# Sevenths for the middle tile: x w_in in a fused retention and two-expert kernel

## The chip, the cores and the metric

One core of one Trainium2 chip. The metric is device time in microseconds (us) for one execution. Everything is float32; the matrix products are made of three float32r products each (below).

## What is computed

A retention layer gives 1536 tokens of width 512. Two feed-forward layers follow. The change lies in the second one, in its first product (`x @ w_in`) and what takes that product's result:

```
def _moe_ref(x, w_a, w_b, w_out):      # x 1536x512, w_a, w_b 512x1536, w_out 1536x512
    return (x @ w_a) * (x @ w_b) @ w_out
def _moe2_ref(x, w_in, w_out):         # x 1536x512, w_in 512x2048, w_out 2048x512
    h = x @ w_in
    g = np.maximum(0.01 * h, h)
    return g @ w_out
x = attention(q, k, v); x = _moe_ref(x, ...); return _moe2_ref(x, ...)
```

## The kernel before

**Tiles.** Everything is held transposed: features on the 128 partitions, 512 tokens along the free axis. The tokens form three tiles, t = 0, 1, 2; t = 1 is the middle one. `y[t, kc]` is x of the second layer (four blocks of 128 features), `w_in` comes in 16 blocks of 128 columns ("wi", f), and `g[t, f]` is the result. Each operand of a product is split into a high and a low float32r part, and `mm3` makes three matmuls: high by high, high by low, low by high. Each matmul loads its own 128x128 weights. SBUF tiles of 128x512 come from a pool of 83 (`Slots`).

**Pairs.** From f = 2 on, blocks of `w_in` are taken in seven pairs, one pair in each round q = 1 to 7 (f = 2q, 2q + 1). In `seven_for_eight` the tiles 0 and 2 are the two rows of a 2x2 block product (features in two halves, columns in two blocks), done in Winograd's way with seven block products for eight. Each is six matmuls of 512 columns; they gather in the PSUM banks `top`, `left` and `mid`. Sums of inputs are formed beforehand (`SY` for x, the "twisted" weights for w_in). The middle tile goes the plain way: `middle` makes 12 matmuls of 512 columns for each of the two blocks, in the banks `pa` and `pb`. A pair has 66 matmuls of 512 columns.

**Order.** `seven_for_eight` is a generator in three parts. In round q the program writes out: the first part of pair q (half of `pa`), the third part of pair q - 1, one product of the next stage (`make2`: six matmuls of 512 columns and six of 256, into three banks `blk` that are held until round 7), and the second part of pair q. Between the products it calls `pump`, which takes work from a queue (rounding of weights, splits, sums of weights, operand forms of the next stage) by nominal cost until the stated time is used up. Every engine executes in the order in which the program writes out, so `pump` decides what stands ahead of what on VectorE and ScalarE.

**Who reads PSUM.** ScalarE copies `top` before the next product is added on the same bank (`s1` L1419, `uu` L1442, `u3` L1431), and makes g by a leaky ReLU (`leaky`, lines 1387 and 1389). VectorE adds `left` and `mid` to earlier copies (`total`, L1423); the ReLU of such sums is done later by `summed`. For the middle tile before, `straight` makes g from `pa` and `pb` at once, two ScalarE instructions of 256 columns each.

**Room.** g tiles that would not fit are sent to DRAM by POOL (`Away.send`, L776) and brought back by SP (L790). This holds for t = 2, and for f from 8 on. Rounding a weight block takes three ScalarE instructions (lines 327, 329, 331) and three of VectorE.

Of the kernel before, what the change touches and what calls it, by code (L numbers as in the profile page):

```python
# [20 lines left out]
P = 128  # L21
# [34 lines left out]
FORM2 = ((), (0,), (1,), (2,), (3,), (4,), (5,), (6, 7))  # L56
MAKE2 = ((), (0,), (1,), (2,), (3,), (4,), (5,), (6, 7))
NMADE2 = 8
LEAD1 = 4
PARK = (0, 0, 0, 0, 0, 1, 1, 1, 2, 1, 1, 2)  # L60
WITH = ((), (), (), (0,), (1,), (2,), (3,), (4,), (5,), (6,), (7, 8, 9), (10, 11))
# [169 lines left out]
def retention_moe_kernel(ctx: ExitStack, tc: tile.TileContext, ins, out):  # L231
# [14 lines left out]
    def as32(t):  # L246
        return t.bitcast(F32)
# [144 lines left out]
        queue.extend(items[2:])  # L392

    def enqueue_split(key, keep=False, far=False):
        def high():
            weights[key] = slots.new(F32R, f"{key[0]}{key[1]}h"), slots.new(F32R, f"{key[0]}{key[1]}l")
            (nc.vector.tensor_copy if key[0] == "wi" and key[1] > 1 else nc.scalar.copy)(weights[key][0], rounded[key])

        def low():
            src = rounded.pop(key)  # L400
            if far:
                nc.scalar.mul(weights[key][1], as32(weights[key][0]), -1.0)
                nc.gpsimd.dma_start(weights[key][1], src, accum_op=ALU.add)
            else:
                nc.vector.tensor_sub(weights[key][1], src, as32(weights[key][0]))
            if keep:
                kept[key] = src
            else:
                slots.done(1)

        behind.extend([(0.05, high), (0.05 if far else 0.61, low)])
# [42 lines left out]
    def twisted(key):  # L454
        return ("t" + key[0], key[1])
# [372 lines left out]
    def seven_for_eight(ka, kb, X, S, xf, ends):  # L828
# [58 lines left out]
        slots.done(4)  # L887
        slots.tick()

    def fast(f):  # L890

        mul, add = nc.vector.tensor_mul, nc.vector.tensor_add
        for t in range(NTILE):
            h[t, f] = slots.new(F32, f"h{t}{f}")
        u = []

        def uu(top):
            u.append(slots.new(F32, f"u{f}"))
            nc.scalar.copy(u[0], top)

        def mb(pb):
            mul(h[1, f], h[1, f], pb)
# [12 lines left out]
        return seven_for_eight(("a", f), ("b", f), x, S, xf, (  # L915
            lambda top: nc.scalar.copy(h[0, f], top),
            lambda left: add(h[0, f], h[0, f], left),
            lambda pa: signed(h[1, f], pa, 1),
            uu,
            lambda top: nc.scalar.copy(h[2, f], top),  # L920
            lambda mid: add(h[2, f], h[2, f], mid),
            mb, c21, c12,
        ))

    y = {}

    def once(cache, kind, f):

# [369 lines left out]
    def y_leave(i, o, parts, with_, op, banks):  # L1298
        sums = banks
        if op:  # L1300
            sums = {m: slots.new(F32, f"yc{i}{o}{m}") for m in parts}
            for m in parts:
                op(sums[m], with_[m], banks[m])

        def onto(d, x):
            nc.gpsimd.dma_start(yf[d], yf[x], accum_op=ALU.add)

        def leave_part(m):
            y_split(i, o, m, sums[m])
            while turn:  # L1310
                t, n = turn.pop(0)
                nc.scalar.mul(yf[t, n], yf[t, n], -1.0)
                if n < 2:
                    onto((2, 2 + n), (2, n))
                    onto((2, n), (0, n))
            if m == 2 and o and not i:
                for j in range(2):
                    onto((0, j), (2, 2 + j))
            if m < 2:
                if not op:  # L1320
                    yf[0, m] = slots.new(F32, f"yf{m}")
                    nc.scalar.copy(yf[0, m], sums[m])
                else:
                    yf[2 * i, 2 * o + m] = sums[m]
                    if i:
                        turn.append((2, 2 * o + m))
                    else:
                        onto((0, 2 + m), (0, m))
            elif op:
                slots.done(1)  # L1330

        for m in parts:
            if op and len(parts) == 3:

                queue.append((0.65, lambda m=m: leave_part(m)))
            else:
                leave_part(m)
# [67 lines left out]
        if f == FF2 - 1:  # L1405
            slots.done(2 * KC)

    sums2 = []

    def summed():  # L1410
        while sums2:
            t, f = sums2.pop(0)
            leaky(g[t, f], g[t, f], t)
            gs.send(t, f)

    def fast2(f):

        def s1(top):
            nc.scalar.copy(g_new(0, f), top)  # L1419
            summed()  # L1420
# [12 lines left out]

        def c21(top):
            straight(2, f, top)
            summed()

        return seven_for_eight(("wi", f), ("wi", f + 1), y, SY, yf, (
            s1,
            lambda left: total(0, f, left),  # L1440
            lambda pa: straight(1, f, pa),
            lambda top: nc.scalar.copy(g_new(0, f + 1), top),  # L1442
            u3,
            lambda mid: total(2, f + 1, mid),
            lambda pb: straight(1, f + 1, pb),
            c21,
            lambda mid: total(0, f + 1, mid),
        ))
# [42 lines left out]
            z.soon.clear()  # L1491

    spare.extend(mixed_items(yf, SY, "r", True))
    before = None
    for q in range(HALF):
        f = 2 * q
        for key in (("wi", f + 2), ("wi", f + 3)) if q + 1 < HALF else ():
            if key in dram:
                obtain(key)
            if key not in rounded:  # L1500
                enqueue_round()
            enqueue_split(key, q + 1 in PAIRS)
        forms = list(FORM2[q])
        for n in range(max(NWQ[q], len(forms))):
            if n < NWQ[q]:
                enqueue_round()
            if n < len(forms):
                queue.append((0.0, lambda m=forms[n]: queue.__setitem__(slice(0, 0), z.items(m))))
        queue.extend(behind)
        behind.clear()  # L1510
        if q + 1 in PAIRS:
            queue.extend(sub_items(("wi", f + 2), ("wi", f + 3)))
        if q in PAIRS:
            now = fast2(f)
            next(now)
            if before:
                next(before, None)
            make2(MAKE2[q - 1])
            next(now)
            before = now  # L1520
            if q == HALF - 1:
                for m in range(LEAD):
                    queue.append((0.34, lambda m=m: z.early(m)))
                queue.extend(z.items(NMADE2))
                next(now, None)
                slots.done(16 + 6 * KC)
# [118 lines left out]
```

## Time and profile before

| | us |
|---|---|
| median of 3 runs | 556.27 (555.9 to 557.31) |
| the profiled execution | 555.79 |
| its span on the core | 554.0 |
| TensorE busy in the span | 548.2 (99%) |
| VectorE, ScalarE busy | 460.3 (83%), 385.8 (70%) |

The pairs of the second layer run from 330 to 448 us of the span. The profile's busy TensorE counts from a matmul's start to its modelled end; the distance between starts shows its pace. The chain of work that ended last is TensorE for 93% of the span.

### The profile page before, as it was taken

How to read it: one execution, taken by the hardware profiler on the slowest of the kernel's cores; microseconds unless marked ns; L12 is line 12 of the kernel's file. 1: busy time of each engine (PE TensorE's matmuls, PEld its weight loads, DVE VectorE, ACT ScalarE, POOL GpSimd, SP SyncE). 2: the span in 40 equal slices, each digit the busy share in tenths (PEclk: the TensorE clock that was granted, in tenths of full speed). 3: DMA queues.
4: the chain of work that ended last, by engine and by line, in shares of the span. 5: the costliest groups of instructions: out<-in, count | busy, mean ns of one | idle time of the engine just before them, and what ended most of it. 6: DMA issues, size and time to landing. Idle time of an engine off the chain costs nothing.

```text
span 554.0 us, 10490 instructions
## 1 busy us (share of the span) xinstructions
PE 548.2 (99%) x3742; PEld 462.0 (83%) x3742; DVE 460.3 (83%) x973; ACT 385.8 (70%) x797; POOL 157.3 (28%) x202
## 2 busy tenths in 40 slices
PE   8999999999999999999999999999999999999997
PEld 5878888888888888788888888888888888888886
DVE  4978968888898898898779869896977798999862
ACT  4876477787779888867657557769766886687800
POOL 3435101113232331266620230221433556600000
PEclk9999999999999999999999999999999999999999
DMA  8999834548698987899993362665777799964111
GB/s 308 353 359 239 214 95 133 155 133 213 175 259 236 243 234 237 269 305 236 234 189 96 57 134 76 180 182 164 240 232 228 209 272 241 222 165 119 59 58 57
DMA packets 49765, 108.19 MB, mean 195 GB/s; under 512 B 5936, under 2 KB 13360, under 8 KB 49712
## 3 DMA queue, kind: packets, MB, share of 16 engines
q1 hardware_dynamic: 27504, 66.80, 36.6%
q0 software_dynamic: 22064, 40.64, 34.4%
q8 instruction: 29, 0.48, 0.3%
q14 instruction: 24, 0.20, 0.1%
q10 hardware_dynamic: 144, 0.08, 0.1%
HBM read 73.68 MB, written 18.35 MB: 166 GB/s over the span
## 4 chain that ended last, share of the span: by engine, by line
PE 93%; DMA 4%; ACT 1%; DVE 0%; SPq 0%; issue 0%
PE blk L259 12%; PE blk L258 12%; PE blk L260 12%; PE top L258 6%; PE top L259 6%; PE top L260 5%; PE pa L258 4%; PE pa L260 4%; PE pa L259 4%; PE pb L258 4%; PE pb L260 4%; PE pb L259 4%; PE mid L258 3%; PE mid L260 3%; PE mid L259 3%; DMA n<-in_kn 2%
## 5 line engine op out<-in xcount | busy, mean ns | idle before, releaser
L259 PE MATMUL blk<-form,form 128*128 128x512 f32 (+1 forms) x224 | 75.8, 339 | 0.0
L258 PE MATMUL blk<-form,form 128*128 128x512 f32 (+1 forms) x224 | 75.6, 337 | 0.0
L260 PE MATMUL blk<-form,form 128*128 128x512 f32 (+1 forms) x224 | 75.3, 336 | 0.0
L174 DVE TENSOR_TENSOR form<-g,form 128x512 fp32r<-128x512 f32 x112 | 57.7, 553 | 1.0 <-DMA out<-c 0.2
L259 PE MATMUL blk<-forma,forma 128*128 128x512 f32 (+1 forms) x168 | 56.9, 338 | 0.0
L258 PE MATMUL blk<-forma,forma 128*128 128x512 f32 (+1 forms) x168 | 56.7, 337 | 0.0
L168 ACT CAST form<-g 128x512 fp32r<-128x512 f32 x112 | 52.3, 513 | 6.1 <-DVE form L174 3.8
L260 PE MATMUL blk<-forma,forma 128*128 128x512 f32 (+1 forms) x168 | 56.4, 336 | 0.0
L174 DVE TENSOR_TENSOR forma<-h,forma 128x512 fp32r<-128x512 f32 x84 | 43.1, 553 | 5.7 <-ACT forma L168 4.0
L258 PEld LDWEIGHTS blk<-form,form 128*128 128x128 f32 x224 | 42.5, 190 | 5.3
L259 PEld LDWEIGHTS blk<-form,form 128*128 128x128 f32 x224 | 42.5, 190 | 4.7
L260 PEld LDWEIGHTS blk<-form,form 128*128 128x128 f32 x224 | 42.3, 189 | 4.8
L168 ACT CAST forma<-h 128x512 fp32r<-128x512 f32 x84 | 38.9, 511 | 8.3 <-DMA h<-h 8.3
L776 POOL DMA_DIRECT2D farg<-g x26 | 15.7, 617 | 79.6 <-ACT g L1389 61.7
L147 POOL DMA_DIRECT2D h<-h x33 | 32.8, 1131 | 15.1 <-DVE h L906 4.9
L258 PEld LDWEIGHTS blk<-forma,forma 128*128 128x128 f32 x168 | 31.9, 190 | 4.0
L259 PEld LDWEIGHTS blk<-forma,forma 128*128 128x128 f32 x168 | 31.9, 190 | 3.6
L260 PEld LDWEIGHTS blk<-forma,forma 128*128 128x128 f32 x168 | 31.7, 189 | 3.6
L776 POOL DMA_DIRECT2D farh<-h x19 | 11.0, 578 | 74.9 <-DVE h L906 50.6
L174 DVE TENSOR_TENSOR form<-wq,form 128x256 fp32r<-128x256 f32 x56 | 23.6, 421 | 10.0 <-ACT form L168 9.9
L168 ACT CAST form<-wq 128x256 fp32r<-128x256 f32 x56 | 22.6, 404 | 5.1 <-PE blk L259 2.4
L147 POOL DMA_DIRECT2D g<-farg x22 | 22.1, 1054 | 7.7 <-DVE form L174 5.1
(3061 smaller groups left out, 1679.5 us busy)
## 6 DMA issues: line engine op xcount, KB each, us to landing
raw_wi<-in_w SPq DMA_DIRECT2D x16, 512.0 KB, 4.4
raw_wq<-in_w SPq DMA_DIRECT2D x16, 512.0 KB, 4.8
farg<-g POOLq DMA_DIRECT2D x26, 256.0 KB, 4.4
g<-farg SPq DMA_DIRECT2D x26, 256.0 KB, 6.7
raw_a<-in_wab SPq DMA_DIRECT2D x12, 512.0 KB, 4.1
raw_b<-in_wab SPq DMA_DIRECT2D x12, 512.0 KB, 4.7
raw_wo<-in_wo SPq DMA_DIRECT2D x12, 512.0 KB, 4.7
g<-farg POOLq DMA_DIRECT2D x20, 256.0 KB, 8.7
```

The lines of the kernel that those rows point to most:

```text
L147: queue.append((0.0, lambda piece=piece: self.nc.gpsimd.dma_start(self.A(*d[1:], j)[piece], self.A(*x1[1:], j)[piece], accum_op=ALU.add)))
L168: nc.scalar.copy(h, src)
L174: nc.vector.tensor_sub(*todo.pop(0))
L258: nc.tensor.matmul(ps, w[0], x[0], start=first, stop=False, skip_group_check=more)
L259: nc.tensor.matmul(ps, w[0], x[1], start=False, stop=False, skip_group_check=more)
L260: nc.tensor.matmul(ps, w[1], x[0], start=False, stop=last, skip_group_check=more)
L776: nc.gpsimd.dma_start(self.far[t, f], self.tiles[t, f])
```

## The change

In rounds q = 2 to 7 the middle tile is done in Winograd's way as well, by itself: its 512 tokens are the two rows of the 2x2 product, 256 each. Its seven products are six matmuls of 256 columns each, in banks `intop`, `inleft` and `inmid`; they replace the 24 matmuls of `middle`. The second block of a pair is then used in one half only, so its high and low parts share one tile. The middle tile's fp32 values (`ym`) are kept until sums of them are formed and split (`inner_items`). Its results are now sums, so the ReLU comes late: `in_c21` does it at the end of the pair, for all sums waiting. Six tiles of g (t = 0, 1 and f = 5, 6, 7) go to DRAM and are recalled in rounds 5 (f = 5) and 7 (f = 6, 7).

```
+INNER = 2
+LENT = {5: 5, 6: 7, 7: 7}
     def enqueue_split(key, keep=False, far=False):
+        part = slice(QT, TT) if key[0] == "wi" and key[1] % 2 and key[1] > 2 * INNER else slice(0, TT)
...
+    def inner_items(last):
...
+    def seven_in_all(ka, kb, ends, inner):
...
+        want(*ka)
+        in_top = bank("intop")[:, 0:QT]
+        product(in_top, ka, 0, token(X0, 0), True, False)
+        ms1(in_top)
+        yield
+        top, left = bank("top"), bank("left")
+        product(top, ka, 0, [y[0, 0], y[0, 1]], True, False)
+        s1(top)
+        product(left, ka, 1, [y[0, 2], y[0, 3]], True, False)
+        pump(2.0)
+        c11(left)
+        left = bank("inleft")[:, 0:QT]
+        product(left, ka, 1, token(X1, 0), True, False)
+        mc11(left)
+        pump(0.7)
+        until(lambda: not ym)
...
+        product(in_top, tb, 1, SM[2], False, True)
+        muu(in_top)
+        product(top, tb, 1, [SY[2, 0], SY[2, 1]], False, True)
+        uu(top)
+        mid = bank("mid")
+        product(mid, ta, 0, [SY[1, 0], SY[1, 1]], True, False)
+        m1(mid)
+        in_mid = bank("inmid")[:, 0:QT]
+        product(in_mid, ta, 0, SM[1], True, False)
+        mm1(in_mid)
+        pump(3.3)
+        product(in_top, tb, 0, SM[3], False, True)
+        mc22(in_top)
+        product(top, tb, 0, [SY[3, 0], SY[3, 1]], False, True)
+        pump(0.6)
+        c22(top)
...
+        pump(0.7)
+        yield
+        product(in_mid, kb, 1, SM[4], False, True)
+        pump(0.6)
+        mc12(in_mid)
+        product(mid, kb, 1, [SY[4, 0], SY[4, 1]], False, True)
+        pump(1.3)
+        c12(mid)
+        product(in_top, ta, 1, token(X1, 1), False, True)
+        mc21(in_top)
+        product(top, ta, 1, [y[2, 2], y[2, 3]], False, True)
+        c21(top)
+        pump(1.0)
...
             elif op:
-                slots.done(1)
+                ym[i, o] = sums[m]
+            else:
+                ym[i, o] = slots.new(F32, "ym")
+                nc.scalar.copy(ym[i, o], sums[m])
...
+    def sent(t, f):
+        gs.send(t, f)
+        if t < 2 and f in LENT:
+            lent[t, f] = park.tile([P, TT], F32, tag=f"lent{t}{f}", name=f"lent{t}{f}")
+            nc.gpsimd.dma_start(lent[t, f], g.pop((t, f)))
+            slots.done(1)
+    def recall(f):
+        for t in range(2):
+            nc.sync.dma_start(g_new(t, f), lent.pop((t, f)))
     def summed():
         while sums2:
             t, f = sums2.pop(0)
             leaky(g[t, f], g[t, f], t)
-            gs.send(t, f)
+            sent(t, f)
+        while sums3:
+            f, i = sums3.pop(0)
+            bend(g[1, f][:, i * QT:(i + 1) * QT], g[1, f][:, i * QT:(i + 1) * QT], i)
...
+        def in_c21(ps):
+            bend(part(f, 1), ps, 1)
+            summed()
+            for i in range(2):
+                sent(1, f + i)
...
         if q in PAIRS:
+            for n in LENT:
+                if LENT[n] == q:
+                    recall(n)
+            if q == INNER:
+                while spare:
+                    spare.pop(0)[1]()
+                queue[0:0] = inner_items(True)
             now = fast2(f)
```

## Rows read from the trace of the kernel before

**Rows 1.** The page: busy time by engine, and the clock in 40 slices.

```profile
PE 548.2 (99%) x3742; PEld 462.0 (83%) x3742; DVE 460.3 (83%) x973; ACT 385.8 (70%) x797; POOL 157.3 (28%) x202
...
PEclk9999999999999999999999999999999999999999
```

**Rows 2.** Waits of PE, whole span: us in total, times, longest; the longest.

```profile
PE warm L986 <- PEq L1634: 0.8, 1, 0.8
```

**Rows 3.** Busy time of one round (q = 3), by engine; clock, DMA share, GB/s.

```profile
363.95:381.01 17.06, 17.06 (x81) 14.23 (x79) 14.13 (x30) 11.78 (x24) 3.01 (x5) 1.00 0.52 143
```

**Rows 4.** Timeline of PE: start, duration, instruction; a stretch of 512 columns.

```profile
349.64 0.39 PE L258 MATMUL pa<-y10h,wi4h 128*128 128x512 f32 x1
...
361.88 0.39 PE L258 MATMUL blk<-form,form 128*128 128x512 f32 x1
```

**Rows 5.** Timeline of PE: 18 matmuls of 256 columns, then of 512.

```profile
307.28 0.28 PE L258 MATMUL blk<-forma,forma 128*128 128x256 f32 x1
...
309.43 0.40 PE L258 MATMUL blk<-forma,forma 128*128 128x512 f32 x1
...
310.82 0.39 PE L258 MATMUL blk<-forma,forma 128*128 128x512 f32 x1
```

**Rows 6.** Tile blk: weight loads, ns min/median/max.

```profile
L258 PEld LDWEIGHTS blk<-form,form x224: 187/188/192, 344.6 to 550.3; 128*128 128x128 f32 x112
```

**Rows 7.** Timeline of PE at the turn to the last round (q = 7).

```profile
426.04 0.39 PE L258 MATMUL pa<-y00h,wi14h 128*128 128x512 f32 x1
...
429.89 0.39 PE L260 MATMUL mid<-r41h,wi13l 128*128 128x512 f32 x1
...
436.30 0.39 PE L258 MATMUL top<-r20h,twi15h 128*128 128x512 f32 x1
```

**Rows 8.** Timeline of ACT at the same turn; in brackets idle before and its releaser.

```profile
426.24 0.38 ACT L1387 ACTIVATE g<-pb 128x256 f32<-128x256 f32 x1 [0.24 <-PE pb L260]
426.52 0.38 ACT L1389 ACTIVATE g<-pb 128x256 f32<-128x256 f32 x1
426.78 0.66 ACT L327 ACTIVATE wq<-raw_wq 128x512 f32<-128x512 f32 x1
...
431.53 0.61 ACT L1389 ACTIVATE g<-top 128x512 f32<-128x512 f32 x1
432.02 0.65 ACT L1389 ACTIVATE g<-g 128x512 f32<-128x512 f32 x1
432.54 0.69 ACT L327 ACTIVATE wq<-raw_wq 128x512 f32<-128x512 f32 x1
...
435.47 0.62 ACT L1419 COPY g<-top 128x512 f32<-128x512 f32 x1
```

**Rows 9.** Timeline of ACT at the turn to round 6.

```profile
409.72 0.66 ACT L327 ACTIVATE wi<-raw_wi 128x512 f32<-128x512 f32 x1
...
413.37 0.57 ACT L1389 ACTIVATE g<-top 128x512 f32<-128x512 f32 x1
...
416.72 0.59 ACT L1419 COPY g<-top 128x512 f32<-128x512 f32 x1 [0.38 <-PE top L260]
```

**Rows 10.** VectorE adds out of PSUM, ns min/median/max: 512 columns, 256 columns.

```profile
L1423 DVE TENSOR_TENSOR g<-g,mid x14: 678/682/689, 341.8 to 446.0; 128x512 f32<-128x512 f32 x14
...
L1472 DVE TENSOR_TENSOR c<-up,blk x4: 414/420/422, 517.3 to 551.0; 128x256 f32<-128x256 f32 x4
```

**Rows 11.** Timeline of DVE: the idle stretch of round 1, the sum of the last turn.

```profile
332.65 0.43 DVE L345 TENSOR_SCALAR wq<-wq 128x512 f32<-128x512 f32 x1 [3.08 <-ACT wq L327]
...
433.12 0.68 DVE L1423 TENSOR_TENSOR g<-g,mid 128x512 f32<-128x512 f32 x1
```

**Rows 12.** DMA issues, KB, median us to landing.

```profile
farg<-g POOLq DMA_DIRECT2D x26, 256.0 KB, 4.4
g<-farg SPq DMA_DIRECT2D x26, 256.0 KB, 6.7
```

**Rows 13.** The SP queue's own waits, 300 to 500 us: total, times, longest.

```profile
SPq L464 <- DMA farg<-g: 17.0, 2, 12.9
```

More of the change, by code (lines that the diff above doesn't have):

```diff
@@ L394, in enqueue_split @@
     def enqueue_split(key, keep=False, far=False):
+        part = slice(QT, TT) if key[0] == "wi" and key[1] % 2 and key[1] > 2 * INNER else slice(0, TT)
         def high():
-            weights[key] = slots.new(F32R, f"{key[0]}{key[1]}h"), slots.new(F32R, f"{key[0]}{key[1]}l")
-            (nc.vector.tensor_copy if key[0] == "wi" and key[1] > 1 else nc.scalar.copy)(weights[key][0], rounded[key])
+            if part.start:
+                both = slots.new(F32R, f"{key[0]}{key[1]}")
+                weights[key] = both[:, 0:QT], both[:, QT:]
+            else:
+                weights[key] = slots.new(F32R, f"{key[0]}{key[1]}h"), slots.new(F32R, f"{key[0]}{key[1]}l")
+            (nc.vector.tensor_copy if key[0] == "wi" and key[1] > 1 else nc.scalar.copy)(
+                weights[key][0], rounded[key][:, part]
+            )
         def low():
@@ L404, in low @@
             else:
-                nc.vector.tensor_sub(weights[key][1], src, as32(weights[key][0]))
+                nc.vector.tensor_sub(weights[key][1], src[:, part], as32(weights[key][0]))
             if keep:
@@ L888, in seven_for_eight, with minus_both, high, low @@
         slots.tick()
+    def inner_items(last):
+        sub, add = nc.vector.tensor_sub, nc.vector.tensor_add
+        def minus_both(d, a, b):
+            nc.vector.scalar_tensor_tensor(d, a, -1.0, b, op0=ALU.mult, op1=ALU.subtract)
+        for op, d, a, b in (
+            (minus_both, (1, 1), (1, 0), (1, 1)), (sub, (1, 0), (0, 0), (1, 0)),
+            (add, (0, 0), (0, 0), (1, 1)), (add, (0, 1), (0, 1), (0, 0)),
+        ) if not last else ():
+            yield 0.69, lambda op=op, d=d, a=a, b=b: op(ym[d], ym[a], ym[b])
+        for n, key in ((3, (1, 0)),) if last else ((1, (1, 1)), (2, (0, 0)), (4, (0, 1))):
+            def high(n=n, key=key):
+                if n == 3:
+                    SM[n] = [tuple(part[:, QT:] for part in y[1, j]) for j in range(2)]
+                else:
+                    hi, lo = slots.new(F32R, f"m{n}h"), slots.new(F32R, f"m{n}l")
+                    SM[n] = [(hi[:, c], lo[:, c]) for c in (slice(0, QT), slice(QT, TT))]
+                for j in range(1 + (n == 3)):
+                    c = slice(j * QT, (j + 1) * QT) if n == 3 else slice(0, TT)
+                    nc.scalar.copy(SM[n][j][0] if n == 3 else hi, ym[key][:, c])
+                SM[n, 0] = None if n == 3 else (hi, lo)
+            def low(n=n, key=key):
+                whole = SM.pop((n, 0))
+                src = ym.pop(key)
+                if whole:
+                    nc.vector.tensor_sub(whole[1], src, as32(whole[0]))
+                else:
+                    for j in range(2):
+                        hi, lo = SM[n][j]
+                        nc.vector.tensor_sub(lo, src[:, j * QT:(j + 1) * QT], as32(hi))
+                slots.done(1)
+            yield 0.05, high
+            yield 0.69, low
@@ new lines, in seven_in_all, with product, token @@
+    def seven_in_all(ka, kb, ends, inner):
+        s1, c11, uu, m1, c22, c21, c12 = ends
+        ms1, mc11, muu, mm1, mc22, mc21, mc12 = inner
+        ta, tb = twisted(ka), twisted(kb)
+        X0, X1 = ([y[1, 2 * i + j] for j in range(2)] for i in range(2))
+        def product(ps, key, half, xs, first, more):
+            w = weights[key]
+            for j in range(2):
+                at0 = j * P if key == kb else half * QT + j * P
+                c = slice(at0, at0 + P)
+                mm3(ps, (w[0][:, c], w[1][:, c]), xs[j], first and j == 0, j == 1, more)
+        def token(parts, i):
+            return [tuple(part[:, i * QT:(i + 1) * QT] for part in pair) for pair in parts]
+        want(*ka)
[14 more added lines that the diff above has]
+        until(lambda: not ym)
+        while ym:
+            spare.pop(0)[1]()
+        until(lambda: ta in weights and ka not in kept)
+        product(in_top, tb, 1, SM[2], False, True)
[14 more added lines that the diff above has]
+        c22(top)
+        slots.done(4)
+        slots.tick()
+        pump(0.7)
[11 more added lines that the diff above has]
+        pump(1.0)
+        slots.done(3)
+        slots.tick()
@@ L923, in fast @@
         ))
-    y = {}
+    y, ym, SM = {}, {}, {}
     def once(cache, kind, f):
@@ L1329, in leave_part @@
             elif op:
-                slots.done(1)
+                ym[i, o] = sums[m]
+            else:
+                ym[i, o] = slots.new(F32, "ym")
+                nc.scalar.copy(ym[i, o], sums[m])
         for m in parts:
@@ L1406, in h2_step @@
             slots.done(2 * KC)
-    sums2 = []
+    sums2, sums3, lent = [], [], {}
+    def sent(t, f):
[3 more added lines that the diff above has]
+            nc.gpsimd.dma_start(lent[t, f], g.pop((t, f)))
+            slots.done(1)
+    def recall(f):
+        for t in range(2):
+            nc.sync.dma_start(g_new(t, f), lent.pop((t, f)))
     def summed():
@@ L1413, in summed, with bend @@
             leaky(g[t, f], g[t, f], t)
-            gs.send(t, f)
+            sent(t, f)
+        while sums3:
+            f, i = sums3.pop(0)
+            bend(g[1, f][:, i * QT:(i + 1) * QT], g[1, f][:, i * QT:(i + 1) * QT], i)
+    def bend(d, src, i):
+        if i:
+            nc.scalar.activation(d, src, AF.Prelu, scale=-0.01, alpha=100.0)
+        else:
+            nc.scalar.activation(d, src, AF.Prelu, alpha=0.01)
     def fast2(f):
@@ L1436, in c21, with part, in_total, in_copy @@
             summed()
+        def part(f, i):
+            return g[1, f][:, i * QT:(i + 1) * QT]
+        def in_total(f, i, ps):
+            nc.vector.tensor_add(part(f, i), part(f, i), ps)
+            sums3.append((f, i))
+        def in_copy(f, i, ps):
+            if (1, f) not in g:
+                g_new(1, f)
+            nc.scalar.copy(part(f, i), ps)
+        def in_c21(ps):
[3 more added lines that the diff above has]
+                sent(1, f + i)
+        if f >= 2 * INNER:
+            return seven_in_all(("wi", f), ("wi", f + 1), (
+                s1,
+                lambda left: total(0, f, left),
+                lambda top: nc.scalar.copy(g_new(0, f + 1), top),
+                lambda mid: nc.scalar.copy(g_new(2, f + 1), mid),
+                lambda top: total(2, f + 1, top),
+                c21,
+                lambda mid: total(0, f + 1, mid),
+            ), (
+                lambda ps: in_copy(f, 0, ps),
+                lambda ps: in_total(f, 0, ps),
+                lambda ps: in_copy(f + 1, 0, ps),
+                lambda ps: in_copy(f + 1, 1, ps),
+                lambda ps: in_total(f + 1, 1, ps),
+                in_c21,
+                lambda ps: in_total(f + 1, 0, ps),
+            ))
         return seven_for_eight(("wi", f), ("wi", f + 1), y, SY, yf, (
@@ L1493, in retention_moe_kernel @@
     spare.extend(mixed_items(yf, SY, "r", True))
+    spare.extend(inner_items(False))
     before = None
@@ L1513, in retention_moe_kernel @@
         if q in PAIRS:
+            for n in LENT:
[3 more added lines that the diff above has]
+                while spare:
+                    spare.pop(0)[1]()
+                queue[0:0] = inner_items(True)
             now = fast2(f)
@@ L1525, in retention_moe_kernel @@
                 next(now, None)
-                slots.done(16 + 6 * KC)
+                slots.done(16 + 6 * KC + 6)
                 slots.tick()
```

## The prediction, as put on record

> **What bounds the kernel.** I read the page first: TensorE is busy 99% of the span, and the granted clock stands at the top digit in all 40 slices, so the 2.4 GHz level holds throughout [rows 1]. A busy matmul row could still hide waits, so I then asked for the waits of TensorE: they come to under 3 us in the whole span, the longest 0.8 us at the start [rows 2], none in the second layer. In one round of the pairs TensorE is busy for all 17.06 us, VectorE for 14.13, ScalarE for 11.78 [rows 3]. So TensorE's own pace sets the time, and two questions decide the change: how much shorter its sequence gets, and whether another engine, now waiting on TensorE, makes it wait.
>
> **TensorE's sequence.** The pace is read between starts. 54 matmuls of 512 columns lie between the two rows of [rows 4]: (361.88 - 349.64)/54 = 0.2267 us each. The 256-column ones: 18 take 309.43 - 307.28 = 2.15 us, and the six of 512 behind them take 1.39 instead of 1.36 [rows 5]. So a run of n costs about 0.12n, plus 0.02 for its two ends. Check: a round has 72 of 512 (66 of the pair, six of the next stage) and one run of six: 72 x 0.2267 + 0.74 = 17.06, which is [rows 3].
> Removed per pair: 24 x 0.2267 = 5.44 us. Added: 42 of 256 columns, in the order written out three runs of twelve (1.46 each) and one of six (0.74), 5.12 us. Gain 0.32 per pair. Over six pairs, with the runs at the first and last pair that stand alone (25 runs, 252 matmuls): 144 x 0.2267 - 252 x 0.12 - 25 x 0.02 = 32.64 - 30.74 = **1.90 us**. This is all that there is to win.
>
> The Trainium skill (TensorE: Matmul & The Clock Gate, section Back-to-back issue gap) says that in a stream of load-and-multiply pairs the spacing is set by both, and gives some 81 ns at 128 and 131 ns at 512 columns. A straight line between these, an estimate from that page, puts 256 columns at 98 ns, three quarters of a long one; then 42 short ones cost more than 24 long ones, and the pair would lose 1 us instead of gaining. This kernel's rows disagree: 0.12 against 0.2267 is 0.53.
>
> **ScalarE, where the sums come late.** Before, the middle tile takes four instructions of 256 columns per pair. After: three copies, one ReLU from PSUM, three ReLUs of sums, seven in all. Their number matters less than their place. `in_c21` first handles its own bank, then calls `summed`, and no other call before it in the pair finds anything: the three 512 sums that were spread over s1, u3 and c21 now stand there too, with the three of 256. I lay out ScalarE from E, the start of the next pair's first product (426.04 for the last round [rows 7]), to s1, the copy of `top` that the next product on `top` must wait for. `pump` takes the same items in the same order (0.6, 1.3, 1.0, 1.8 as before), so the durations are those of [rows 8], start to start.
> Last round (q = 7, which pumps four roundings): first copy, ready 0.92 after E by six short matmuls and a latency as in [rows 8], ends at 1.2. Two roundings and a form, 426.78 to 431.53: 4.75, to 5.95. The burst: 0.28 from PSUM, three of 512 at 0.53, three of 256 at 0.28 (spacing of the pb pair, spacing of the 512 rows): 2.71, to 8.66. c21 0.49, to 9.15. Third rounding and form, 432.54 to 435.47: 2.93, to 12.08. s1: 0.62, done at **12.7**.
> TensorE reaches the product that needs s1 at: run of twelve 1.46, mid 1.36, in_top 0.74, top 1.36, next-stage product 2.10, top 1.36, left 1.36, run of twelve 1.44 = **11.18**. So it waits 1.5 us, once. Before, s1 ended at 435.47 + 0.62 = 436.09 and the product began at 436.30 [rows 7, 8]: 0.2 us to spare already.
> Rounds 3 to 6 pump two roundings of w_in and one of w_out, no form before s1: [rows 9] give 3.65 for two, so 1.83 for one. 1.2 + 3.65 + 2.71 + 0.49 + 1.83 + 0.6 = 10.5 against 11.18: 0.7 us to spare, no wait. The row shows that s1 was even 0.38 early before. Round 2 has no burst ahead of it; the two n = 3 splits (0.6) fit.
> Bounds for the wait of the last round: zero, if a form slips behind s1 (1.1 us less) and the burst overlaps better; 3.4 if the recalled tiles come late (below). I take 1.5, the sum of rows.
>
> **VectorE.** Added per pair: three sums of 256 out of PSUM at 0.42 [rows 10] = 1.26 us. Taken off: half a subtraction (0.69 to 0.42 by the same ratio) and part of a cast (0 to 0.42). Net 0.6 to 1.0 us in 17.06 with 2.9 idle [rows 3]. c22 is wanted only by the product on `top` at E + 3.5 and c12 only by banks and by the burst, so this hides; without that cover it would be up to 1 us per pair. The four sums and three splits of `ym` (some 4.5 us) go into rounds 0 and 1, where VectorE stood idle before 332.65 for 3.08 us [rows 11] and a little before that; what does not fit pushes the round-1 work back by about 1 us, and that work feeds products 6 us on. The extra ScalarE copy in the first layer's last stage: 0.6 us, its forms are made some products ahead. Each of these I take as 0; none can gain.
>
> **Tiles and DMA.** By the tile counts in the code, the six split tiles of x add 6, late g tiles of the middle add 2 from round 4, shared weight tiles take off 2, the lent ones take off 6 until recalled: room is about as before in rounds 4 to 6, and some six tiles less once all are back in round 7. Twelve more transfers of 256 KB, of a kind that takes 4.4 and 6.7 us to land [rows 12], hide at a DMA share of 0.52 [rows 3]. What may not hide is a recall that waits for a tile: SP's fetch of w_out already waited 12.9 us for a tile that a store was leaving [rows 13]. If the recalled f = 6 tiles are issued only at E, they land at E + 6.7; the form wants them at 4.85 (1.2 and two roundings). Then ScalarE, and s1 with it, is late by 1.9 more: 3.4 in all.
>
> **Sum.** 555.79 - 1.90 + 1.5 = 555.4 for the profiled execution, which ran 0.48 below the median; against the median 556.27 - 0.4 = **555.9**. A difference under 0.3% (1.7 us) can't be told from no change.
>
> **Rivals.**
> A, the forecast: one wait in round 7, net -0.4; own range -1.2 to +0.5. Chance 0.42.
> B, no wait anywhere: 556.27 - 1.90 = 554.4. For it: ScalarE idles in every round (5.3 of 17.06 us [rows 3]); against it: the 0.2 us of spare in the last round. Chance 0.33.
> C, slower: recalled tiles land late in round 7, as in the part on tiles. Price 3.4 us of waiting, net +1.5: 557.8. It decides once the wait passes 1.9, that is once the form waits 0.4 for its data. For it: [rows 13]; against it: SP has nothing else to issue then, and an early free tile would let it run ahead. Chance 0.12.
> D, slower in every pair: the burst ends later because its third 512 sum waits for VectorE. c12 ran at 433.12, 3.2 us behind the last matmul of its bank at 429.89 [rows 7, 11], where ScalarE would want it at about E + 6.2 (1.2 + 3.65 + 0.28 + 1.06). That lag uses up the 0.7 us; each further us costs one in each of five rounds: -0.4 + 5 = +4.6, 560.9. Against it: the new order writes c12 out one `pump(1.0)` earlier. Chance 0.12.
> F, short matmuls paced by their weight loads: 0.188 us each [rows 6] instead of 0.12, 252 x 0.068 = 17 us more, 573. It is the skill's rule above taken to its end; [rows 5] rule it out for runs of the same shape. Chance 0.01.
>
> **Chances and range.** Faster by over 0.3%: most of B (0.28) and a tail of A (0.02): 0.30. Slower by over 0.3%: D, F and half of C: 0.19. The rest, 0.51, within. Range 554.0 to 558.4: it cuts off D, F, and a few hundredths of B's fast and C's slow end.
>
> **What would show it.** TensorE: 42 starts 0.12 apart per pair, round length 16.74 instead of 17.06; a length above that is a wait, and the waits of TensorE name it. Round 7: a wait before the first product of `top` with twisted weights, released by ScalarE's copy at s1. ScalarE: seven ReLUs in a row at the end of each pair. If TensorE waits in rounds 3 to 6 as well, D is right and my 0.7 us was wrong; if the wait of round 7 is behind a form that waits for a DMA, C; if there is none, B, and the layout of ScalarE failed.

## The result and the profile after

The changed kernel takes 559.95 us (median of 4 runs, 559.66 to 560.27) against 556.11 for the kernel before in the same series (4 runs): ratio 1.0065, 95% interval 1.0047 to 1.0082. It is slower by 3.8 us, and the prediction, 555.9 with a range to 558.4, was wrong. (The 556.27 that the prediction started from is the median of the first three of those four runs.) The profiled execution has a span of 558.5 us, 4.5 more than before.

The page of the changed kernel: span, busy time by engine, granted clock in 40 slices, and the chain of work that ended last.

```profile
span 558.5 us, 10797 instructions
...
PE 549.0 (98%) x3850; PEld 465.1 (83%) x3850; DVE 467.7 (84%) x1000; ACT 392.9 (70%) x821; POOL 160.4 (29%) x208
...
PEclk9999999999999999999999999999999999999999
...
PE 86%; ACT 5%; DMA 4%; DVE 3%; issue 1%; SPq 0%; DVEq 0%; ACTq 0%
```

The clock is as before [rows 1] and busy TensorE hardly differs. What is new is that ScalarE and VectorE stand in the chain that sets the end, where TensorE alone had 93%. The waits of TensorE within the pairs say where (us in total, times, longest); before there was none there [rows 2]. Line numbers are each kernel's own. In the changed kernel L1561 is `s1`, ScalarE's copy of `top`. L1565 is VectorE's sums out of the banks of 512 columns: `c11` out of `left`, `c22` out of `top`, `c12` out of `mid`. L1584 is its sums for the middle tile: `mc11` out of `inleft`, `mc22` out of `intop`, `mc12` out of `inmid`. L329 to L333 are ScalarE's part of a rounding, and L170 and L176 are the halves on ScalarE and VectorE of an operand form for the next stage.

```profile
PE top L260 <- ACT g L1561: 1.4, 1, 1.4
PE inmid L260 <- DVE g L1565: 0.9, 2, 0.5
PE intop L260 <- DVE g L1584: 0.9, 2, 0.5
```

Rounds q = 2 to 6 of the changed kernel, each from its first product on `top` to that of the next (length, then busy us of PE, PEld, DVE, ACT and POOL, clock, DMA share, GB/s); the second line answers to [rows 3].

```profile
347.38:365.91 18.53, 17.54 (x98) 14.66 (x97) 16.17 (x37) 14.11 (x29) 3.56 (x5) 1.00 0.70 206
365.91:382.65 16.74, 16.74 (x98) 14.76 (x97) 15.11 (x33) 12.72 (x29) 3.47 (x5) 1.00 0.52 162
382.65:401.04 18.39, 17.54 (x99) 14.67 (x98) 14.64 (x33) 14.00 (x30) 7.32 (x12) 1.00 0.91 294
401.04:417.78 16.74, 16.74 (x99) 14.76 (x98) 15.10 (x34) 12.76 (x28) 5.50 (x9) 1.00 0.70 211
417.78:434.52 16.74, 16.74 (x99) 14.77 (x98) 12.79 (x29) 12.55 (x28) 4.68 (x8) 1.00 0.79 248
```

Rounds 3, 5 and 6 last 16.74 us, 0.32 less than before, as worked out. Rounds 2 and 4 last 18.53 and 18.39: 1.79 and 1.65 more than 16.74, so more than the gain of all six pairs is lost in them. ScalarE is busy for 14.0 and 14.1 us in these two and for 12.6 to 12.8 in the others; the list `NWQ = (0, 1, 2, 1, 2, 1, 1, 4)`, blocks of w_out rounded in each round, has a 2 at just these places.

In the timeline of TensorE of the changed kernel the three kinds of wait are the matmuls with a bracket (idle before it, and what released it).

```profile
389.35 0.39 PE L262 MATMUL mid<-r11h,twi8l 128*128 128x512 f32 x1
390.13 0.39 PE L260 MATMUL inmid<-m1h,twi8h 128*128 128x256 f32 x1 [0.39 <-DVE g L1565]
390.35 0.28 PE L261 MATMUL inmid<-m1l,twi8h 128*128 128x256 f32 x1
...
396.50 0.39 PE L260 MATMUL intop<-y10h,twi8h 128*128 128x256 f32 x1 [0.46 <-DVE g L1584]
...
438.58 0.28 PE L262 MATMUL intop<-m2h,twi15l 128*128 128x256 f32 x1
440.29 0.50 PE L260 MATMUL top<-r20h,twi15h 128*128 128x512 f32 x1 [1.44 <-ACT g L1561]
```

The bracket is short of the loss, for a busy time overlaps the next start: `inmid` begins 0.78 us behind the matmul before it where the pace is 0.23, so 0.55 is lost, and the matmul behind it comes 0.22 later, not 0.12, another 0.10. Counted so, by distances between starts above the pace, the pairs lose 0.21 at the turn of round 1, 1.74 in round 2 (`inmid` 0.80, `intop` 0.72, `top` 0.22), 1.59 in round 4 and 1.70 in round 7: 5.24 us (5.27 in the table below, which adds before rounding). Less the 1.90 gained that makes +3.3. The rest of the +4.5 is mostly 0.87 by which this execution is late already at its first pair (330.73 against 329.86); that mark differs between executions, as the table below shows, and the median went up by 3.8 only.

Why is `inmid` late? The timeline of VectorE in round 4 (changed kernel); `c11` is the line at 389.39, `mc22` the one at 396.03, `c22` the one at 396.69:

```profile
388.26 0.43 DVE L176 TENSOR_TENSOR form<-wq,form 128x256 fp32r<-128x256 f32 x1 [1.45 <-ACT form L170]
388.78 0.69 DVE L176 TENSOR_TENSOR form<-g,form 128x512 fp32r<-128x512 f32 x1
389.39 0.68 DVE L1565 TENSOR_TENSOR g<-g,left 128x512 f32<-128x512 f32 x1
389.99 0.42 DVE L1584 TENSOR_TENSOR g<-g,inleft 128x256 f32<-128x256 f32 x1
...
396.03 0.41 DVE L1584 TENSOR_TENSOR g<-g,intop 128x256 f32<-128x256 f32 x1
396.69 0.68 DVE L1565 TENSOR_TENSOR g<-g,top 128x512 f32<-128x512 f32 x1
```

and of ScalarE ahead of it:

```profile
382.94 0.40 ACT L1556 ACTIVATE g<-g 128x256 f32<-128x256 f32 x1
383.25 0.58 ACT L1511 ACTIVATE g<-top 128x512 f32<-128x512 f32 x1
...
385.55 0.57 ACT L1561 COPY g<-top 128x512 f32<-128x512 f32 x1
386.02 0.67 ACT L329 ACTIVATE wq<-raw_wq 128x512 f32<-128x512 f32 x1
...
387.85 0.38 ACT L170 CAST form<-wq 128x256 fp32r<-128x256 f32 x1
```

and the same two instructions, ScalarE's half of the form and VectorE's `c11`, in the timelines of the kernel before:

```profile
385.43 0.38 ACT L168 CAST form<-wq 128x256 fp32r<-128x256 f32 x1
...
386.98 0.68 DVE L1423 TENSOR_TENSOR g<-g,left 128x512 f32<-128x512 f32 x1
```

The burst (the ReLUs of the sums, one behind the other, at the end of the pair before) ends at 383.25, and s1 (385.55) is in time, as forecast. Behind it stands the second rounding of the round (from 386.02), and behind that ScalarE's half of an operand form, at 387.85. VectorE's half stands ahead of `c11` in the written order and holds VectorE for 1.45 us; `c11`, the only reader of `left`, ends at 390.07, and `inmid` starts at 390.13. Counted from the round's first product on `top` (382.65, before 381.01), ScalarE's form is at 5.20 and was at 4.42, and `c11` is at 6.74 and was at 5.97, behind the same form: 0.77 later. The same holds in round 2 (form 5.35 against 4.42), where no burst is ahead; there a copy and two splits of `ym` come new onto ScalarE.

Before, nobody wanted the bank of `left` so soon. The program has eight PSUM banks. Before, a round used `pa`, `pb`, `top`, `left`, `mid` and the three held `blk`: eight. Now it uses `intop`, `inleft`, `inmid`, `top`, `left`, `mid` and three: nine, so the ninth, `inmid`, gets the one that `c11` drains in the same round, and wants it at 6.93 (389.58, the pace behind 389.35). Both have to come together: a `c11` as early as before would have ended at 5.97 + 0.68 = 6.65, 0.28 in time.

`intop` waits for `mc22`, a sum that the kernel before did not have, and `top` behind it for `c22`; both stand behind all the queue's work. From 388.26 to 396.44 VectorE is busy for 7.84 of 8.18 us. The same stretch before, from the same form on (385.85 to 394.03), was exactly as full, and TensorE waited for nothing. So over round 4 VectorE has 3.75 us of idle time, but 3.38 of it lie ahead of the form; behind the form next to nothing can be made up.

### The profile page after: what moved, and what is told of

Read it like the earlier page. It is cut to its first block, busy times and chain, and to the rows that moved or that the text cites. A ratio compares the mean times of both kernels' runs of the same rounds, so it can differ in the third digit from the quotient of the medians.

```text
span 558.5 us, 10797 instructions
## 1 busy us (share of the span) xinstructions
PE 549.0 (98%) x3850; PEld 465.1 (83%) x3850; DVE 467.7 (84%) x1000; ACT 392.9 (70%) x821; POOL 160.4 (29%) x208
## 4 chain that ended last, share of the span: by engine, by line
PE 86%; ACT 5%; DMA 4%; DVE 3%; issue 1%; SPq 0%; DVEq 0%; ACTq 0%
PE blk L261 12%; PE blk L260 12%; PE blk L262 12%; PE top L260 5%; PE top L261 5%; PE top L262 5%; DMA n<-in_kn 3%; PE pa L260 3%; PE pa L262 3%; PE pa L261 3%; PE pb L260 3%; PE pb L262 3%; PE pb L261 3%; PE mid L260 2%; PE mid L261 2%; PE mid L262 2%
## 5 line engine op out<-in xcount | busy, mean ns | idle before, releaser
L176 DVE TENSOR_TENSOR form<-g,form 128x512 fp32r<-128x512 f32 x112 | 58.0, 557 | 0.7
L170 ACT CAST form<-g 128x512 fp32r<-128x512 f32 x112 | 52.4, 512 | 7.5 <-DMA g<-g 3.9
L176 DVE TENSOR_TENSOR forma<-h,forma 128x512 fp32r<-128x512 f32 x84 | 43.2, 556 | 3.6 <-issue 2.2
L170 ACT CAST forma<-h 128x512 fp32r<-128x512 f32 x84 | 38.9, 510 | 4.7 <-DMA h<-h 4.7
L176 DVE TENSOR_TENSOR form<-wq,form 128x256 fp32r<-128x256 f32 x56 | 23.7, 423 | 12.1 <-ACT form L170 12.1
L170 ACT CAST form<-wq 128x256 fp32r<-128x256 f32 x56 | 22.6, 403 | 7.2 <-DVE wq L192 4.8
```

Of the source, the lines that this page charges most:

```text
L170: nc.scalar.copy(h, src)
L176: nc.vector.tensor_sub(*todo.pop(0))
```

## The experiments

All are given against the kernel before, run on the same chip in the same series. Its median was 556.58 (14 runs) for e1, e2, e3 and b1, 556.39 (29 runs) for b2, e5, x1 and x2, 556.30 (29 runs) for x3, x4 and x5, and 556.11 for the changed kernel ("after"), as above; so kernels of different series are to be compared by their ratios. Span, first pair and late are read from one execution each. "First pair" is the start of the first product on `top` in round 1, "late" the sum of distances between TensorE's starts above the pace, from there to 453 us.

| kernel | median | ratio (95%) | span | first pair | late |
|---|---|---|---|---|---|
| before | | | 554.0 | 329.86 | 0 |
| after | 559.95 | 1.0065 (1.0047 to 1.0082) | 558.5 | 330.73 | 5.27 |
| e1_spread | 561.81 | 1.0087 (1.0069 to 1.0106) | 560.5 | 330.86 | 7.29 |
| e2_c11_first | 558.05 | 1.0038 (1.0024 to 1.0052) | 558.1 | 331.52 | 4.17 |
| e3_rounding_moved | 558.95 | 1.0043 (1.0028 to 1.0058) | 557.4 | 331.41 | 3.56 |
| b1_burst_only | 557.28 | 1.0018 (1.0007 to 1.0030) | 555.4 | 330.22 | 0.98 |
| b2_lent_only | 556.51 | 1.0004 (0.9993 to 1.0014) | 554.8 | 330.45 | 0 |
| e5_less_ahead | 558.78 | 1.0046 (1.0030 to 1.0063) | 556.0 | 329.53 | 4.01 |
| x1_rounds_0_1 | 556.48 | 1.0004 (0.9993 to 1.0015) | 553.9 | 329.89 | 1.63 |
| x2_round_1 | 556.88 | 1.0021 (1.0008 to 1.0035) | 555.1 | 330.20 | 2.47 |
| x3_sums_sooner | 556.53 | 1.0005 (0.9995 to 1.0015) | 554.1 | 330.50 | 1.15 |
| x4_three_last | 556.74 | 1.0013 (1.0001 to 1.0024) | 554.9 | 330.36 | 2.14 |
| x5_both | 555.84 | 0.9995 (0.9984 to 1.0006) | 554.0 | 329.81 | 1.80 |

In every row but those of b1 and b2, which have no sevenths for the middle tile, span - 554.0 is (first pair - 329.86) + late - 1.90 within 0.3 us: e2 1.66 + 4.17 - 1.90 = 3.93 against 4.1, x5 -0.05 + 1.80 - 1.90 = -0.15 against 0.0. For b1 and b2 it holds without the 1.90: b1 0.36 + 0.98 = 1.34 against 1.4. So, to within 0.3 us, the gain of 1.90 is there in all, and waits are the rest.

**The burst on ScalarE, alone.** The kernel before with the sums' ReLU taken out of s1 and u3, so that all stands at c21:

```
         def s1(top):
             nc.scalar.copy(g_new(0, f), top)
-            summed()
         def u3(top):
             nc.scalar.copy(g_new(2, f + 1), top)
-            summed()
```

> The kernel before, with summed called in c21 alone (its calls in s1 and u3 taken out), so that three ReLUs of 512 columns stand in one place at the end of a pair and the rest is as it was. Theory (the place of the ReLUs alone makes s1 late in the last round): ScalarE has two more of 0.53 us ahead of s1 in round 7, where 0.2 us was to spare, so TensorE waits about 0.85 us there and nowhere else; total 0.85 above before, 557.0. Rival (without the new banks and products the order does no harm): no wait, 556.1.

Its one wait in the pairs, in the last round (TensorE's timeline of b1_burst_only):

```profile
437.55 0.50 PE L258 MATMUL top<-r20h,twi15h 128*128 128x512 f32 x1 [0.72 <-ACT g L1419]
```

0.88 us lost, 0.10 more on the matmul behind it, and +0.70 in the median, where 0.85 was expected. In the kernel before, the burst (of three ReLUs) makes s1 late where four blocks are rounded, and nowhere else.

**Part of the burst taken earlier.** The ReLUs of the sums then waiting are done at `mm1`, in mid pair:

```
-                lambda ps: in_copy(f + 1, 1, ps),
+                lambda ps: (in_copy(f + 1, 1, ps), summed()),
```

> The changed kernel, with one more call of summed, right behind the ScalarE copy mm1, so that the leaky ReLU of c11's sum and of mc11's sum (0.53 and 0.28 us) is done there, where ScalarE idles some 2.5 us, and not in the burst at the end of the pair; nothing on VectorE or TensorE changes. Theory (ScalarE's order: its burst at the pair's end makes s1 late in round 7, and in rounds 2 and 4, which round two blocks of w_out, it reaches the operand forms late, on which VectorE waits ahead of c11, whose bank inmid wants): the 1.6 us wait of round 7 shrinks to about 0.8, the waits of round 4 (1.6 in all) to 0.8 or less, round 2 (no burst ahead of it) keeps its 1.7; total about 558.3. Rival (VectorE simply has too much work in rounds 2 and 4): round 4 keeps its 1.6, only round 7 gains 0.8; total 559.1.

It helped in round 4 (`inmid` no longer waits, 0.91 late instead of 1.59), so the burst is what makes the form late there. It did not in round 2, which has no burst ahead of it: 1.98, where it was 1.74 (e5 below, whose edit acts in round 7 alone, has 1.98 there too, so 0.24 is scatter between executions). And round 7 got worse: 2.76 where 0.8 was expected, and the total is above both forecasts. That is a miss. ScalarE (timeline of e1_spread) stands still there before the second rounding:

```profile
429.29 0.76 ACT L333 ACTIVATE sl<-raw_wq 128x512 uint16<-128x512 uint32 x1
431.57 0.66 ACT L329 ACTIVATE wq<-raw_wq 128x512 f32<-128x512 f32 x1 [1.52 <-issue]
```

The profile names nothing that it waited for. But a store of a g tile to DRAM, issued by POOL, landed at 431.50, 5.31 us after its issue, and the rounding began 0.07 behind that:

```profile
426.19 0.54 POOL L786 DMA_DIRECT2D farg<-g  x1 [4.86 <-ACT g L1509]
```

In this trace ScalarE's queue, too, stands at L329 until 431.53, for a semaphore that this landing sets. So the new `wq` tile most likely took the room that the store was leaving. This is inferred from the times; no run tested it. The four runs spread over 2.2 us (560.11 to 562.32). What followed on TensorE is told in the last section.

**c11 ahead of the queue's work.**

```
-        pump(2.0)
         c11(left)
+        pump(2.0)
```

> The changed kernel with VectorE's sum c11 written out right behind its product, ahead of the queue's 2.0 us of work and not behind it. Theory (nine banks are wanted of eight, and inmid gets the bank that c11 drains): the waits ahead of inmid in rounds 2 and 4 (0.8 and 0.65 us) vanish; the waits ahead of intop for mc22 stay between 0.3 and 1.0 each, since the forms ahead of it still wait for ScalarE; round 7 keeps its 1.6; total 558.6 to 559.4. Rival (VectorE has too much work): what inmid gains is lost again ahead of intop, total 559.9 as before.

The waits of TensorE within the pairs of e2_c11_first:

```profile
PE intop L260 <- DVE g L1584: 1.5, 2, 0.9
PE top L260 <- ACT g L1561: 1.4, 1, 1.4
```

The line of `inmid` is gone in both rounds: this shows that its bank hung on `c11`, and `c11` on what was queued ahead of it. The work is still there, though, and more is lost behind `mc22`: 1.41 and 1.04 in rounds 2 and 4, on `intop` and the matmuls behind it (`top` for `c22` among them), where it was 0.94 in each. So 0.57 of the 1.45 gained on `inmid` is lost again, part of what the rival said. In all 4.17 late instead of 5.27; the ratio is 1.0038 instead of 1.0065, and the intervals overlap a little. The total is 0.5 us below the range expected.

**The second rounding moved from round 4 to round 1.**

```
-NWQ = (0, 1, 2, 1, 2, 1, 1, 4)
+NWQ = (0, 2, 2, 1, 1, 1, 1, 4)
```

> The changed kernel with one rounding of a w_out block moved from round 4 to round 1 (two, two, one, one in rounds 1 to 4). Theory (the second rounding, three ScalarE instructions of 1.83 us together and three of VectorE, is what makes rounds 2 and 4 late): the 1.6 us of waits in round 4 vanish, rounds 2 and 7 keep their 1.7 each; total 558.3. Rival (the waits are of the new products themselves or of tiles running short): round 4 keeps its waits, total 559.9.

Round 4 loses nothing any more, and round 2, where the form now stands behind `c11` (355.17 behind 354.24) and doesn't hold VectorE, 0.30. So both waits come with that rounding; that round 2 would gain as well was not expected. But round 1, which took the rounding, loses 0.47 instead of 0.21, and round 3 has a new wait, 1.07, on s1. ScalarE (timeline of e3_rounding_moved) at the turn to it:

```profile
366.19 0.63 ACT L1509 ACTIVATE g<-g 128x512 f32<-128x512 f32 x1 [1.85 <-DVE g L1565]
...
369.96 0.56 ACT L1561 COPY g<-top 128x512 f32<-128x512 f32 x1
```

This is the mechanism of rival D: the third ReLU of the burst waits for `c12` on VectorE, and s1 is late with it. In the changed kernel the same idle is there in round 4, without reaching s1:

```profile
400.49 0.64 ACT L1509 ACTIVATE g<-g 128x512 f32<-128x512 f32 x1 [1.20 <-DVE g L1565]
```

**Less work ahead of s1 in round 7.** The third rounding and its form go behind s1:

```
-    def make2(ns):
+    def make2(ns, us=1.8):
...
-            pump(1.8)
+            pump(us)
...
-            make2(MAKE2[q - 1])
+            make2(MAKE2[q - 1], 0.0 if q == HALF - 1 else 1.8)
```

> The changed kernel with the 1.8 us of queue work behind the next-stage product taken out in round 7 alone, so that ScalarE's third rounding and a form (2.9 us) stand behind s1 and not ahead of it. Theory (round 7 waits because of what stands ahead of s1 on ScalarE): the wait of 1.6 us at s1 vanishes, at most 0.5 comes back ahead of inmid or intop, as the form now stands between s1 and c11; rounds 2 and 4 keep 1.7 and 1.6; total 558.4 to 558.9. Rival (tiles or recalls are late in round 7): the wait stays, 559.9.

The 1.70 of round 7 become 0.42, and no wait on s1 is left; rounds 2 and 4 keep 1.98 and 1.59. The ratio is 1.0046, where it was 1.0065.

**The lent tiles, alone.** The kernel before with `LENT`, `sent` and `recall` of the diff, nothing else:

```
+LENT = {5: 5, 6: 7, 7: 7}
...
+            for n in LENT:
+                if LENT[n] == q:
+                    recall(n)
```

> The kernel before with one part of the change alone: the six g tiles lent to DRAM and recalled in rounds 5 and 7. Theory (the transfers hide): no wait of TensorE in the pairs, time as before within 0.3 us. Rival (the recall holds up the form of f = 6, and s1 behind it): up to 1.9 us of waiting in round 7, 558. If the stretch ahead of the first pair, where the changed kernel is 0.9 us later than the one before, is later here too, then it is the DRAM tiles and not the new instructions that shift it.

No wait in the pairs, 556.51 against 556.39: lending costs nothing that can be measured. The DMA issues of the changed kernel (count, KB, median us to landing) agree:

```profile
lent<-g POOLq DMA_DIRECT2D x6, 256.0 KB, 4.1
g<-lent SPq DMA_DIRECT2D x6, 256.0 KB, 3.8
```

**All repairs together.** x1_rounds_0_1 has the edits of e1, e2 and e5 and rounds w_out earlier; x2_round_1 has those of e2 and e5 alone, with three roundings in round 1:

```
-NWQ = (0, 1, 2, 1, 2, 1, 1, 4)
+NWQ = (1, 2, 1, 1, 1, 1, 1, 4)     # x1_rounds_0_1
+NWQ = (0, 3, 1, 1, 1, 1, 1, 4)     # x2_round_1
```

> All the remedies together: c11 ahead of the queue work, ReLUs of c11 and mc11 behind mm1, less ahead of s1 in round 7, and the second roundings of rounds 2 and 4 moved to rounds 0 and 1. Theory (the waits come of order alone on ScalarE and VectorE, and the sequence of TensorE is 1.9 us shorter): waits of TensorE in the pairs 1.0 us or less in all instead of 5.3, total 555.6 to 556.3, no slower than before. Rival (VectorE's added work has no room anywhere): 2 us or more of waits stay in other rounds, 557 or more.

> The same, without the ReLUs behind mm1, and with both second roundings moved to round 1, which then has three. Theory: no wait in rounds 2 and 4; in round 3 the burst may wait for c12 on VectorE and s1 with it, up to 1.0 us as in the run that moved one rounding; total 556 to 557. Rival (VectorE has no room): 2 us or more of waits, 557 or more.

x1 is back at the time before, 0.2 us above the range expected: 1.63 late instead of 1.0 or less, 0.94 of it on `intop` in round 7, where `mc22` stands behind the fourth rounding. x2 has 1.66 on `intop` in round 2, where none was expected, and 0.33 there on `top` for s1: three roundings in round 1 push the queue into the next one.

**The sums sooner, and one rounding less at the end.** x3_sums_sooner is x1 with less work ahead of `mc22` and more behind c22; x4_three_last is x1 with another list; x5_both is both.

```
-        pump(3.3)
+        pump(2.4)
...
-        pump(0.7)
+        pump(1.6)
...
-NWQ = (1, 2, 1, 1, 1, 1, 1, 4)
+NWQ = (1, 3, 1, 1, 1, 1, 1, 3)     # x4_three_last, x5_both
```

> The run with all remedies, and 0.9 us of the queue's work moved from ahead of mc22 to behind c22. Theory (what waits are left, 0.36 us in round 2 and 0.94 in round 7, stand ahead of intop because mc22 is behind queue work on VectorE): they fall by 0.9 us each, to none in round 2 and 0.1 in round 7; total about 1.2 below the run with all remedies, 555.3. Rival (VectorE has no room): the waits come back ahead of another bank, total 556.5.

> The run with all remedies, and one rounding moved from round 7 to round 1 (three there, three in the last). Theory: mc22 in round 7 no longer stands behind a rounding that waits for ScalarE, its 0.94 us of waiting vanishes, the rest stays (0.7 us in rounds 1 and 2, up to 0.5 more in round 1 or 2 from the extra rounding); total 555.5 to 556.2. Rival (no room on VectorE in rounds 1 and 2): 1 us or more of new waits in round 2, 556.5 or more.

> Both: 0.9 us of queue work from ahead of mc22 to behind c22, and one rounding from round 7 to round 1. Theory: waits of TensorE in the pairs 0.5 us or less in all, so 1.4 us or more of the 1.9 is left; total 554.9 to 555.3, below the kernel before. Rival (no room on VectorE): 1 us or more of waits, 556 or more.

x3 takes most of the wait on `intop` away and leaves 0.83 in round 7, 0.56 of it on `top` for c22, which is now the late one. x4 has no wait in round 7, but 1.93 in round 2, 1.66 of it on `intop`, as x2 had; it differs from x1 in the list alone, so the third rounding in round 1 brings this. x5 has 1.36 in round 2 (1.09 of it on `intop` and on `top` for c22, the rest on `top` for s1) and 0.23 in round 7. In x3 and x4 the rival, no room on VectorE, gave the better number; x5 lies between the two in time, and its 1.8 us of waits are the rival's. The waits of TensorE in the pairs of x5_both, the best of all:

```profile
PE intop L260 <- DVE g L1584: 0.3, 1, 0.3
PE top L260 <- DVE g L1565: 0.2, 1, 0.2
```

555.84 against 556.30 is no difference that these runs can tell (interval 0.9984 to 1.0006). With 1.8 us of lateness left, the 1.90 gained is just used up. So order alone moved 5.27 us of waits down to 1.15 at best (x3), and no order that was tried makes the change pay: most of what is left in rounds 2 and 7 stands behind VectorE's queue.

## Why the prediction was wrong

**TensorE's sequence: right.** 0.32 per pair and 1.90 in all; three rounds show 16.74 to the hundredth. The estimate by a straight line through two figures of the Trainium skill (TensorE: Matmul & The Clock Gate, section Back-to-back issue gap) would have made rounds longer; this trace disagrees, with 0.12 between starts of 256 columns, as [rows 5] had.

**ScalarE's burst: right.** The forecast was s1 done at E + 12.7 and a wait of 1.5 us, once. ScalarE in the last turn of the changed kernel, with E = 427.52:

```profile
428.44 0.37 ACT L1590 COPY g<-intop 128x256 f32<-128x256 f32 x1 [2.45 <-PE intop L262]
...
431.75 0.76 ACT L333 ACTIVATE sl<-raw_wq 128x512 uint16<-128x512 uint32 x1
432.38 0.38 ACT L170 CAST form<-wq 128x256 fp32r<-128x256 f32 x1
432.66 0.92 ACT L170 CAST form<-g 128x512 fp32r<-128x512 f32 x2
433.49 0.38 ACT L1554 ACTIVATE g<-intop 128x256 f32<-128x256 f32 x1
433.77 0.62 ACT L1509 ACTIVATE g<-g 128x512 f32<-128x512 f32 x1
...
435.94 0.41 ACT L1556 ACTIVATE g<-g 128x256 f32<-128x256 f32 x1
436.25 0.58 ACT L1511 ACTIVATE g<-top 128x512 f32<-128x512 f32 x1
...
439.66 0.58 ACT L1561 COPY g<-top 128x512 f32<-128x512 f32 x1
```

The copy ends at 440.24, E + 12.72. The wait was 1.59, with 0.11 behind it; b1 shows that the burst alone makes such a wait, e5 that the work ahead of s1 sets its size. Rounds 3 to 6 have no wait on s1, as said. The 0.7 us of spare was less in truth, for the third ReLU waited 1.2 in round 4; e3 shows what happens when it is used up.

**Tiles and DMA: right.** b2 shows that lending is hidden by itself, and in the fence above the form of g that follows the second rounding (432.66) begins without idle time: the recalled tiles were there. The two tiles of f = 6 that it reads landed at 430.19 and 431.22, 1.4 us ahead of it at the least.

**VectorE: wrong, and this step decided.** "c22 is wanted only by the product on `top` at E + 3.5 and c12 only by banks and by the burst, so this hides", and "Each of these I take as 0". The step left out the two sums that cost most: `c11`, which had no waiting reader before, and `mc22`, which is new. And `c22`, which it named as hidden, cost 0.22 in rounds 2 and 4 each.

It added VectorE's busy time and compared it with its idle time. Over a round that was no shortage: in round 4 VectorE is busy for 14.64 of 18.39 us. What counts is where a sum stands in its order: behind a form that waits for ScalarE (e2 shows it for `c11`), and behind the queue's work, in a stretch without gaps (x3, where less of that work stands ahead of `mc22`, bears this out). The layout of ScalarE stopped at s1, where a delay of up to 0.7 us costs nothing; it was not followed on to the form, where the same delay reaches VectorE. That "the two n = 3 splits (0.6) fit" is the same slip in round 2: s1 was in time, the form was not. It counted SBUF tiles and not PSUM banks, of which the code wants nine in a round. And it looked at a mean round, q = 3, with one rounding of w_out, while the loss lies in the two rounds with two.

Measured: 1.74 + 1.59 us, and 0.21 at the turn of round 1, where 0 stood. With 3.5 more, the forecast -0.4 would have been +3.1, and with 1.70 for 1.5 in round 7 it would have been +3.3; 0.5 of the measured 3.8 is not accounted for by the pairs.

**Rivals.** B (no wait) is refuted by the wait on s1, C (late recalls) by the form at 432.66, F by the pace. D had the right engine and the right kind of delay, but it took the burst for the victim, and every pair for the place: what VectorE held up were PSUM banks, in two rounds. D's own mechanism reached TensorE in e3 alone.

**Open.** The stretch before the pairs ends between 329.53 and 331.52 in the executions profiled. Nothing in the diff explains that: e5, with the whole change, is the earliest, and both b1 and b2, with a part each, are later than the kernel before. In the changed kernel TensorE shows no wait from 300 us to the pairs; a cast on ScalarE that idles for 0.50 us at 69 us, "issue" in the profile, may be part of it, and was not traced further. That nine banks for eight are the reason why `inmid` needs the bank of `left` is read from the code; no run gave it another bank. Nor is the extra 0.10 us behind a wait explained.

## What to carry to other kernels

When a change adds accumulators, count all that are open at once, the held ones too, against the banks; for each bank that is then reused, find the instruction that drains it and what stands ahead of that one in its engine's order. Do this for the round with the most queued work, not for a typical one. A gain of 0.3 us per round in a sequence without gaps is kept only where every instruction that TensorE waits for has that much to spare, and moving queued work about (e2, e3, x2, x4) mostly moved the wait to the next sum in the order.

## What the runs showed of the hardware

In one execution a long wait cost more than itself. In e1_spread TensorE, busy until then, stood still for 2.6 us. First the granted clock (window, columns as above), then the timeline:

```profile
440.83:444.30 3.47, 3.47 (x9) 2.78 (x10) 3.40 (x8) 2.54 (x5) 3.47 (x4) 0.53 1.01 278
```

```profile
440.83 0.80 PE L260 MATMUL top<-r20h,twi15h 128*128 128x512 f32 x1 [2.60 <-ACT g L1561]
441.43 0.63 PE L261 MATMUL top<-r20l,twi15h 128*128 128x512 f32 x1
441.85 0.63 PE L262 MATMUL top<-r20h,twi15l 128*128 128x512 f32 x1
...
444.28 0.39 PE L262 MATMUL mid<-r10h,twi14l 128*128 128x512 f32 x1
444.50 0.39 PE L260 MATMUL mid<-r11h,twi14h 128*128 128x512 f32 x1
```

For 3.5 us the clock was at 0.53, the 1.2 GHz level but for the edges: matmuls of 512 columns begin 0.42 to 0.43 us apart, then 0.22 again. The eight steps to 444.28 take 3.45 us where 8 x 0.2267 = 1.81 is the pace, so 1.64 us were lost on top of the 2.76. Behind the wait of 1.44 us in the changed kernel the rows show nothing like it: the next matmul begins 0.34 us later, and the clock of that execution is 1.00. Two of the four executions of e1_spread have a mean clock of 0.997, and they are the slowest two (562.23 and 562.32); the other two, at 1.00, took 560.11 and 561.39. So the clock is part of that spread. That the wait brought the clock down is read from the order of the two; no run tested it.
